# Moving every second one of the first twelve input loads from SyncE's queue to ScalarE's

## The chip, the core and the metric

The kernel runs on one core of a Trainium2 chip. The metric is the device time of one execution in microseconds; the time given for a version is the median of several runs. Beside the times there is one profiled execution, whose trace all durations here come from.

## The reference

Inputs are q, k, v, a_re and a_im, each of shape (4, 8, 768, 48) = (batch B, heads H, sequence S, head size D), and four weight matrices. The first half is a gated linear recurrence, the second half a gated feed-forward layer on its result:

```python
mag = sqrt(a_re**2 + a_im**2);  scale = minimum(mag, 0.999) / (mag + 1e-6)
for t in range(S):
    new_re = ar*S_re - ai*S_im          # ar, ai: a_re*scale, a_im*scale at time t
    new_im = ar*S_im + ai*S_re
    S_re, S_im = new_re + outer(k[t], v[t]), new_im
    y[t] = q[t] @ S_re
x = y, heads side by side: (3072, 384)
out = x + sigmoid(x @ w_res) * ((gelu(x @ w_gate) * (x @ w_val)) @ w_out)
```

w_gate and w_val are 384 x 1536, w_out is 1536 x 384, w_res is 384 x 384. All inputs and the output are float32.

## The kernel before

The sequence is cut into six chunks of 128 positions. A *unit* of work is one chunk of one batch, or the same chunk of two batches: unit 0 is batch 0, chunk 0; unit 1 is batch 1, chunk 0; unit 2 is batches 2 and 3, chunk 0; units 3 and 4 are chunk 1 of batches 0, 1 and of 2, 3; and so on, 14 units in all. For each unit three Python functions record steps:

- `prepare` loads `ar`, `ai`, `q`, `k`, `vf` (one load per batch and tensor, line 366), and takes the complex gates into logarithm and angle. On ScalarE it computes `la = Ln(ar)` (L387) and `t = Exp(-la)` (L388); then `t = t*ai` (L390) and `s = t*t` (L392 on ScalarE or L394 on VectorE), `s = Ln(s+1)` (L395), `la = 0.5*s + la` (L396, VectorE), then lh and ll (L399, L401). The angle is `t = Arctan(t)` (L426). The running sums over the chunk are matmuls with a triangular matrix (L352); an angle carry from the chunk before is added by a small DMA from GpSimd's queue (`t<-fr`, L432 and L438); the split parts are `th` (L327) and `tl` (L445). Sine, cosine and the exponentials follow on ScalarE (L416, L417, L470), then the features of q and k.
- `attend` does the attention-like products (L528, L540) and the state.
- `forward` does the feed-forward layer: the gate and value products on TensorE (L598), gelu on ScalarE (L603), the product on VectorE (L604), the output product (L624) and the store (L633).

A function `weights` records sixteen loads of the weight matrices, which GpSimd issues (L333), casting to bfloat16 on the way.

The steps are not run in the order of recording. `ORDER` is a list, written out by hand, of all step numbers; `Plan.run` walks it and lets each step emit its instruction. Each engine so gets its instructions in this order, and executes them in that order. `PLACE` maps some step numbers to an engine; the function `place(default)` looks up the number of the step that is about to be recorded. `Plan.run` also emits an activation table load for ScalarE (L640) whenever a step needs another table than the one in place. The first such load comes with the first step that computes on ScalarE, step 21, the logarithm of unit 0.

The order begins with loads only:

```python
    16, 97, 98, 17, 181, 178, 179, 294, 293, 410, 180, 411, 296, 295, 21, 22, 102, 103, 104, 105, ...
```

Steps 16 and 17 are `ar` and `ai` of unit 0; 97 and 98 those of unit 1; 178, 179 and 180, 181 those of unit 2 (two batches); 293, 294 are `ar` of unit 3 and 295, 296 its `ai`; 410, 411 are `ar` of unit 4. Steps 21 and 22 are unit 0's logarithm and exponential on ScalarE, 102 and 103 those of unit 1. The next loads after 295 in SyncE's order are 412 and 413 (`ai` of unit 4), 19, 100, 99, 643.

All wide work tiles, the loaded ones among them, share 25 buffers (`WD`). A load of a new tile takes the buffer whose last use lies furthest back in the order, and has to wait for that use. The first fourteen loads take fresh buffers. Load 412, the fifteenth, takes the one that held `s` of unit 0, whose last use is L396 of unit 0.

One load brings 128 positions x 8 heads x 48 floats, 192 KB, in pieces of 192 bytes (one position of one head).

Of the kernel before, what the change touches and what calls it, by code (L numbers as in the profile page):

```python
# [24 lines left out]


PLACE = {
    24: "DVE", 40: "DVE", 50: "DVE", 105: "DVE", 114: "DVE", 116: "POOL", 117: "POOL", 121: "DVE", 129: "ACT", 131: "DVE",
    145: "ACT", 190: "DVE", 213: "DVE", 223: "DVE", 225: "ACT", 230: "ACT", 236: "DVE", 305: "DVE", 306: "DVE", 322: "POOL",
    330: "DVE", 340: "DVE", 342: "ACT", 344: "DVE", 422: "DVE", 446: "DVE", 456: "DVE", 460: "DVE", 463: "ACT", 554: "POOL",  # L30
# [92 lines left out]
class Plan:  # L123
# [10 lines left out]
    def add(self, eng, kind, fn, reads=(), writes=(), size=1, act=None):  # L134
        deps = set()
        for v in reads:
            deps.update(v.writers)
        for v in writes:
            deps.update(v.writers)
            deps.update(v.readers)  # L140
        stores = [v.store for v in list(reads) + list(writes) if v.store is not None]
        stores = sorted(set(stores), key=stores.index)
        t = Step(eng, kind, fn, deps, stores, size, act)
        t.index = len(self.steps)
        for v in writes:
            v.writers, v.readers = [t], []
        for v in reads:
            if t not in v.writers:
                v.readers.append(t)
        for x in stores:  # L150
            x.users.append(t)
        self.steps.append(t)
        return t
# [25 lines left out]
def kernel(  # L179
# [13 lines left out]
    nc = tc.nc  # L193
# [123 lines left out]
    add = plan.add  # L317

    def place(default):

        return PLACE.get(len(plan.steps), default)

# [31 lines left out]
    def flat(t, n):  # L354
        return t[:, 0:n].rearrange("p c h d -> p (c h d)")

    def prepare(p):
        s, n = st[p], size[p]
        N = n * DM

        def load(name, src):
            s[name] = Wide(name, FP)
            parts = []
            for i, (b, c) in enumerate(units[p]):
                def fn(i=i, b=b, c=c):
                    nc.sync.dma_start(out=s[name].tile[:, i], in_=src[b, :, c * 128:(c + 1) * 128, :].rearrange("h t d -> t h d"))  # L366
                v_ = s[name].part()
                add("SP", "load", fn, (), [v_])
                parts.append(v_)
            s[name].writers = [x for v_ in parts for x in v_.writers]  # L370

# [3 lines left out]
        for name, src in (("ar", a_re), ("ai", a_im), ("q", q), ("k", k), ("vf", v)):  # L375
            load(name, src)
# [43 lines left out]
        if units[p][0][1] < NC - 1:  # L420
            add("POOL", "mrd", lambda: nc.gpsimd.dma_start(
                out=s["mr"].tile[0:n * H, 0, :], in_=P2("E")[127:128].rearrange("p c (h d) -> p (c h) d", d=D)), [s["E"]], [s["mr"]])
# [6 lines left out]
        if olds:  # L429
            src = sorted({where[(b, c - 1)] for b, c in units[p]})  # L430
            if len(src) == n == 2 and src[0][0] == src[1][0]:
                add("POOL", "carry", lambda u=src[0][0]: nc.gpsimd.dma_start(  # L432
                    out=F("t")[0:1], in_=st[u]["fr"].tile[127:128].rearrange("p c m -> p (c m)"), accum_op=OP.add), olds, [s["t"]])
            else:
                tp = [s["t"].part() for _ in range(n)]
                for i in range(n):
                    tp[i].writers, tp[i].readers = list(s["t"].writers), list(s["t"].readers)
                    add("POOL", "carry", lambda i=i, u=src[i]: nc.gpsimd.dma_start(  # L438
                        out=F("t")[0:1, i * DM:(i + 1) * DM], in_=st[u[0]]["fr"].tile[127:128, u[1]], accum_op=OP.add), [olds[i]], [tp[i]])
# [9 lines left out]
        for i, (b, c) in enumerate(units[p]):  # L449
            if ST:  # L450
                add("PE", "cumT", lambda i=i: sums(cth[i], i, F("th"), F("tl")), [s["th"], s["tl"]], [cth[i]])
            else:
# [5 lines left out]
                out=T("fr")[:, i], in0=T("fr")[:, i].bitcast(INT), scalar=-TWO_PI, in1=cth[i].tile,  # L458
# [10 lines left out]
        for m, (src, bi) in enumerate((("fr", zero), ("fw", half_pi))):  # L469
            act("sin", lambda m=m, src=src, bi=bi: nc.scalar.activation(  # L470
                out=T("CS")[:, 0:n * H, m, :], in_=P2(src).rearrange("p c (h d) -> p (c h) d", d=D),
                func=AF.Sin, bias=bi, scale=1.0 if m == 0 else -1.0), [s[src]], [cs[m]], "T")

        for g, src, mag in (("Q", "q", "E"), ("K", "k", "Ei")):
            add("DVE", "qe", lambda g=g, src=src, mag=mag: nc.vector.tensor_tensor(
                out=T(g + "e")[:, 0:n * H].rearrange("p x u d -> p (x u d)"), in0=flat(T(src), n),
                in1=P2(mag).rearrange("p c m -> p (c m)"), op=OP.mult), [s[src], s[mag]], [s[g + "e"]], n)
        for g in "QK":
            s[g] = Feat(g)
            add("DVE", "feat", lambda g=g: nc.vector.tensor_tensor(  # L480
                out=s[g].tile[:, 0:n * H, 0:DD].rearrange("p x (u d) -> p x u d", u=2),
                in0=T(g + "e")[:, 0:n * H].to_broadcast([128, n * H, 2, D]), in1=T("CS")[:, 0:n * H], op=OP.mult), [s[g + "e"]] + cs, [s[g]], n)
        s["QT"], s["KT"] = [], []
        for i in range(n):
            for g in "QK":
                s[g + "T"].append(Buf(g + "T"))
                gT = s[g + "T"][i]
                if p >= PE_T:
                    add("SP", "dT", lambda g=g, i=i, gT=gT: nc.sync.dma_start(
                        out=gT.tile, in_=s[g].tile[:, i * H:(i + 1) * H].rearrange("p x d -> p (x d)"), transpose=True), [s[g]], [gT])  # L490
# [180 lines left out]
```

## Time and profile before

| | |
|---|---|
| median of 3 runs | 268.33 us (265.72 to 268.8) |
| profiled execution: time / span on the core | 270.18 us / 268.4 us |
| mean granted TensorE clock | 0.973 |
| PE busy | 229.0 us (85%) |
| VectorE (DVE) busy | 231.7 us (86%) |
| ScalarE (ACT) busy | 218.8 us (82%) |
| GpSimd (POOL) busy | 103.8 us (39%) |
| DMA queue q1 (issued by SyncE) | 157,696 packets, 35.53 MB |
| DMA queue q0 (issued by GpSimd) | 4,448 packets, 3.90 MB |

The span is the time from the first to the last instruction on the core; the execution's own time is 1.8 us longer. "Busy" leaves out the instructions of an engine's sequencer: waiting, branching and issuing DMAs. An engine with a "q" behind its name (SPq, POOLq) is that sequencer. A releaser behind an arrow is what ended a wait.

### The profile page before, as it was taken

To read this page: it belongs to the slowest core of one execution; us is meant where nothing else is said; L and a number is where in the kernel's file an instruction comes from. 1 tells how busy PE (TensorE), PEld (TensorE's weight loads), DVE (VectorE), ACT (ScalarE), POOL (GpSimd) and SP (SyncE) were. 2 spreads that over 40 slices of the span, in tenths; PEclk is the share of its full clock that TensorE was granted. 3 is DMA by queue.
4 is the path that set the end of the run, shared out by engine and by line. 5 is a ranking of instruction groups with operands and counts; after the bars stand their busy time and mean duration, and the time that the engine had idled before them with its cause. 6 is when DMAs were issued, how large, how long until landed. Compare 5 with 4: busy or idle time off the path is not lost.

```text
span 268.4 us, 6355 instructions
## 1 busy us (share of the span) xinstructions
PE 229.0 (85%) x2426; PEld 183.2 (68%) x2426; DVE 231.7 (86%) x398; ACT 218.8 (82%) x356; POOL 103.8 (39%) x125
## 2 busy tenths in 40 slices
PE   0323857498996999999997999988999999999993
PEld 0112646397874988688876777777888868877782
DVE  3689899969996899999998999997999998829273
ACT  6999989778698999998999999998988868651240
POOL 1202247793131953768458855742110001201010
PEclk9999995989997999999999999999999999999999
DMA  8999999999819989977979999767896937420111
GB/s 141 188 185 187 188 179 190 208 180 201 143 26 176 156 140 178 180 159 146 192 178 168 192 186 174 165 106 173 175 186 142 153 72 176 91 56 29 46 62 59
DMA packets 162174, 39.83 MB, mean 148 GB/s; under 512 B 155616, under 2 KB 162144, under 8 KB 162144
## 3 DMA queue, kind: packets, MB, share of 16 engines
q1 hardware_dynamic: 157696, 35.53, 74.7%
q0 software_dynamic: 4448, 3.90, 9.1%
q8 instruction: 19, 0.31, 0.5%
q14 instruction: 11, 0.09, 0.1%
HBM read 31.26 MB, written 4.72 MB: 134 GB/s over the span
## 4 chain that ended last, share of the span: by engine, by line
PE 62%; DMA 15%; ACT 10%; POOL 5%; SPq 4%; issue 3%; DVE 1%; POOLq 0%; DVEq 0%; ACTq 0%
PE pb L598 29%; PE pb L624 14%; DMA ar<-in_a_re_dram 7%; PE pb L352 5%; PE pb L613 4%; SPq L366 4%; DMA t<-fr 3%; PE pb L528 3%; DMA wg<-in_moe_w_gate_dram 3%; PE pb L497 3%; ACT L640 2%; POOL th L327 1%; DMA KT<-fK 1%; ACT t L426 1%; ACT CS L470 1%
## 5 line engine op out<-in xcount | busy, mean ns | idle before, releaser
L598 PE MATMUL pb<-xT,wg 128*128 128x256 bf16 (+1 forms) x504 | 57.5, 264 | 5.8 <-ACT h L603 2.2
L604 DVE SCALAR_TENSOR_TENSOR h<-h,pb 128x512 bf16<-128x512 bf16 (+1 forms) x84 | 48.4, 602 | 16.1 <-ACT h L603 9.4
L603 ACT ACTIVATE h<-pb 128x512 bf16<-128x512 f32 (+1 forms) x84 | 41.0, 545 | 25.6 <-PE pb L598 25.4
L598 PE MATMUL pb<-xT,wv 128*128 128x256 bf16 (+1 forms) x504 | 57.1, 257 | 0.9 <-DMA wv<-in_moe_w_val_dram 0.9
L624 PE MATMUL pb<-wo,h 128*128 128x384 bf16 x288 | 56.2, 326 | 0.0
L640 ACT ACT_TABLE_LOAD x42 | 53.9, 1283 | 1.4 <-PEq L655 0.7
L598 PEld LDWEIGHTS <-wg 128*128 128x128 bf16 x504 | 44.9, 101 | 14.0 <-issue 3.9
L598 PEld LDWEIGHTS <-wv 128*128 128x128 bf16 x504 | 42.3, 98 | 8.2 <-DMA wv<-in_moe_w_val_dram 1.3
L631 POOL TENSOR_TENSOR ot<-ot,x 128x384 f32<-128x384 f32 x18 | 16.5, 921 | 53.6 <-DVE ot L628 41.3
L624 PEld LDWEIGHTS <-h 128*128 128x128 bf16 x288 | 26.5, 97 | 12.9 <-issue 0.5
L531 DVE TENSOR_TENSOR am<-pb,mask 128x512 bf16<-128x512 f32 x48 | 31.8, 681 | 2.3 <-PE pb L528 2.3
L390 POOL TENSOR_TENSOR t<-t,ai 128x768 f32<-128x768 f32 (+1 forms) x9 | 15.6, 1737 | 18.6 <-DMA ai<-in_a_im_dram 13.1
L528 PE MATMUL pb<-QT,KT 96*128 96x128 bf16 x192 | 17.4, 219 | 4.1 <-ACT QT L325 1.7
L352 PE MATMUL pb<-th,ut_one 128*128 128x384 f32 x24 | 11.7, 486 | 8.7 <-POOL th L327 8.7
L327 POOL CAST v<-vf 128x768 bf16<-128x768 f32 (+1 forms) x10 | 8.8, 878 | 23.7 <-DMA vf<-in_v_dram 14.7
L528 PEld LDWEIGHTS <-KT 96*128 96x128 bf16 x192 | 13.1, 97 | 7.1 <-issue 2.3
L445 POOL TENSOR_TENSOR tl<-t,th 128x768 fp32r<-128x768 f32 (+1 forms) x9 | 14.8, 1649 | 7.1 <-ACT th L325 6.8
L327 POOL CAST th<-t 128x768 fp32r<-128x768 f32 (+1 forms) x9 | 10.3, 1152 | 17.7 <-DMA t<-fr 6.2
L613 PE MATMUL pb<-wr,xT 128*128 128x384 bf16 x72 | 16.3, 343 | 0.0
L497 PE MATMUL pb<-ident,fK 128*128 128x128 bf16 x112 | 9.7, 242 | 6.9 <-DVE fK L480 6.9
L540 PE MATMUL pb<-v,am 128*128 128x48 bf16 x192 | 12.5, 186 | 2.8 <-DVE am L531 2.8
L387 ACT ACTIVATE la<-ar 128x768 f32<-128x768 f32 (+1 forms) x14 | 10.4, 759 | 5.5 <-DMA ar<-in_a_re_dram 4.6
(91 smaller groups left out, 484.9 us busy)
## 6 DMA issues: line engine op xcount, KB each, us to landing
ar<-in_a_re_dram SPq DMA_DIRECT2D x24, 192.0 KB, 4.6
ai<-in_a_im_dram SPq DMA_DIRECT2D x24, 192.0 KB, 4.5
k<-in_k_dram SPq DMA_DIRECT2D x24, 192.0 KB, 4.4
q<-in_q_dram SPq DMA_DIRECT2D x24, 192.0 KB, 4.3
vf<-in_v_dram SPq DMA_DIRECT2D x24, 192.0 KB, 4.3
out_dram<-ot SPq DMA_DIRECT2D x24, 192.0 KB, 2.3
wv<-in_moe_w_val_dram POOLq DMA_DIRECT2D x6, 192.0 KB, 6.0
wg<-in_moe_w_gate_dram POOLq DMA_DIRECT2D x6, 192.0 KB, 7.2
```

Of the source, the lines that this page charges most:

```text
L327: on[eng].tensor_copy(out=out, in_=in_)
L352: nc.tensor.matmul(out=bank.tile, lhsT=ut_one, rhs=x[:, i * DM:(i + 1) * DM], start=(j == 0), stop=(j == 1))
L497: nc.tensor.transpose(out=tp.tile[:, h, :], in_=s[g].tile[:, i * H + h], identity=ident)
L528: nc.tensor.matmul(out=ap.tile[:, h, :], lhsT=kT.tile[0:DD, u * H // 2 + h, :], rhs=qT.tile[0:DD, u * H // 2 + h, :], start=True, stop=True)
L531: add("DVE", "am", lambda u=u, am=am, ap=ap: nc.vector.tensor_tensor(out=am.tile[:, u * H // 2:(u + 1) * H // 2, :], in0=ap.tile, in1=mask ...
L598: nc.tensor.matmul(out=o_.tile[:, u, :], lhsT=w_[:, k_, (2 * m + u) * 128:(2 * m + u + 1) * 128], rhs=s["xT"].tile[:, k_, 0:n].rearrange(" ...
L603: add("ACT", "gelu", lambda gp=gp, hv=hv: nc.scalar.activation(out=hv(), in_=gp.tile, func=AF.Gelu), [gp], [hh], n, "G")
L604: add("DVE", "h", lambda vp=vp, hv=hv: nc.vector.scalar_tensor_tensor(out=hv(), in0=hv(), scalar=0.5, in1=vp.tile, op0=OP.mult, op1=OP.mul ...
L613: nc.tensor.matmul(out=rp.tile, lhsT=s["xT"].tile[:, k_, i, :], rhs=wr[:, k_, :], start=(k_ == 0), stop=(k_ == KF - 1))
L624: nc.tensor.matmul(out=op_.tile, lhsT=s["h2"].tile[:, k_, i * 128:(i + 1) * 128], rhs=wo[:, k_, :], start=(k_ == 0), stop=(k_ == NF - 1))
L631: add(e8, "otx", lambda i=i, ot=ot, e8=e8: on[e8].tensor_tensor(out=ot.tile, in0=ot.tile, in1=s["x"].tile[:, i].rearrange("p h d -> p (h d ...
L640: plan.run(ORDER, lambda table: nc.scalar.preload_act_table_set(ACT_SETS[table]))
```

## The change

Of the first twelve loads in the order, the 2nd, 4th, 6th, 8th, 10th and 12th (steps 97, 17, 178, 294, 410, 411) are issued with `nc.scalar.dma_start`, so from ScalarE's instruction stream and on ScalarE's DMA queue. The order list is the same; so are the transfers, the buffers and all other steps.

```diff
 PLACE = {
+    97: "ACT", 17: "ACT", 178: "ACT", 294: "ACT", 410: "ACT", 411: "ACT",
     24: "DVE", 40: "DVE", 50: "DVE", 105: "DVE", 114: "DVE", 116: "POOL", 117: "POOL", 121: "DVE", 129: "ACT", 131: "DVE",
...
             for i, (b, c) in enumerate(units[p]):
-                def fn(i=i, b=b, c=c):
-                    nc.sync.dma_start(out=s[name].tile[:, i], in_=src[b, :, c * 128:(c + 1) * 128, :].rearrange("h t d -> t h d"))
+                eq = place("SP")
+
+                def fn(i=i, b=b, c=c, eq=eq):
+                    (nc.scalar if eq == "ACT" else nc.sync).dma_start(out=s[name].tile[:, i], in_=src[b, :, c * 128:(c + 1) * 128, :].rearrange("h t d -> t h d"))
                 v_ = s[name].part()
-                add("SP", "load", fn, (), [v_])
+                add(eq, "load", fn, (), [v_])
                 parts.append(v_)
```

## The prediction

> **What bounds the kernel now.** I read the page first, its slices above all, then the chain that ended last, then the timeline of the first 16 us, then busy time by stage.
>
> The page, its rows for ACT, DMA and GB/s in 40 slices of 6.7 us:
>
> ```profile
> ACT  6999989778698999998999999998988868651240
> DMA  8999999999819989977979999767896937420111
> GB/s 141 188 185 187 188 179 190 208 180 201 143 26 176 156 140 178 180 159 146 192 178 168 192 186 174 165 106 173 175 186 142 153 72 176 91 56 29 46 62 59
> ```
>
> Up to about 70 us the DMA engines are at nine tenths with 180 to 208 GB/s: the stage is bound by transfers, and ScalarE is at nine tenths beside it. The chain that ended last, in order of time (start, duration, what), shows how the two are linked:
>
> ```profile
> 1.87 0.84 SPq L366
> ...
> 10.89 4.58 DMA ar<-in_a_re_dram
> 15.55 0.84 ACT la L387
> ...
> 38.36 1.81 POOL t L390
> ...
> 44.45 7.86 DMA wg<-in_moe_w_gate_dram
> ...
> 53.44 1.32 PE pb L598 x12
> 55.62 14.28 DMA ar<-in_a_re_dram
> 69.98 0.85 ACT la L387
> ```
>
> The chain runs through SyncE's issues to the twelfth load (10.89), through ScalarE (15.55), GpSimd and the weights that it issues, TensorE's first gate products (53.44) and a load that took 14.28 us. After that it is mostly TensorE.
>
> The timeline from 0 to 16 us (start, duration, engine, line; in brackets the idle time before):
>
> ```profile
> 0.74 1.28 ACT L640 ACT_TABLE_LOAD   x1 [0.74 <-PEq L655]
> 0.74 1.07 SPq L366 DMA_DIRECT2D ar<-in_a_re_dram  x2
> 3.87 0.52 ACT L387 ACTIVATE la<-ar 128x384 f32<-128x384 f32 x1 [1.84 <-DMA ar<-in_a_re_dram]
> 10.89 1.00 SPq L366 DMA_DIRECT2D ar<-in_a_re_dram  x1
> 11.93 4.11 SPq L366 DMA_DIRECT2D ai<-in_a_im_dram  x4
> 15.55 0.84 ACT L387 ACTIVATE la<-ar 128x768 f32<-128x768 f32 x1 [0.54 <-DMA ar<-in_a_re_dram]
> ```
>
> Here the reader sees the main thing: an issue isn't free. SyncE's first two take 0.53 us each, the later ones about 1.03 (4.11 / 4). That is the time in which 192 KB move at 190 GB/s, so the issuing sequencer is held until the engines have taken earlier loads. Busy time by stage (PE, PEld, DVE, ACT, POOL, each with its count, clock, DMA share, GB/s):
>
> ```profile
> 4.00:16.00 12.00, 2.90 (x6) 1.39 (x6) 7.80 (x15) 10.80 (x17) 1.79 (x2) 1.00 1.31 189
> 16.00:28.00 12.00, 4.38 (x16) 2.96 (x17) 11.02 (x19) 11.95 (x18) 1.93 (x2) 1.00 1.37 186
> 54.00:70.00 16.00, 15.14 (x225) 13.69 (x224) 13.03 (x23) 11.28 (x28) 8.85 (x12) 0.93 1.19 192
> 83.00:268.00 185.00, 178.20 (x1901) 142.50 (x1900) 161.31 (x270) 147.34 (x245) 69.82 (x72) 0.99 0.74 140
> ```
>
> ScalarE works 22.75 of the 24 us from 4 to 28: it has next to no room there. After 83 us TensorE has 6.8 us of idle time in 185.
>
> **What the change removes.** Six issues leave SyncE. The transfers stay, and they are what paces SyncE, so I take nothing for this. What SyncE could gain is bounded by ScalarE's waits on `ar` loads, 0.54 us at 15.55 and 2.2 us at 69.98, so 2.8 us in all; at the other end it is nothing.
>
> The Trainium skill, "DMA: Bandwidth & Descriptors", section "Issuing engines are not separate DMA queues", says that DMAs from ScalarE and SyncE run on the same 16 engines and interleave, and that a second issuer only saves issue time, usually small beside the transfer. The first half agrees with the nine tenths above. The second doesn't agree with the 1.03 us of an issue: with issues as small as the rule has them the sum would be that of the second rival, 269.2, in place of 275.3.
>
> **What it adds.** Six issues on ScalarE, all ahead of its first table load and logarithm, since ScalarE works in the order of the list. The trace has no DMA issue on ScalarE, so I bound it by SyncE's rows.
> - Low: all six at the 0.53 us of the first two: 0.74 + 6 x 0.535 = 3.95 us.
> - High: the two sequencers share one line, and ScalarE's sixth issue ends where the twelfth ends now: 10.89 + 1.00 = 11.89 us.
> - Value: two quick issues, then four held back. With two queues sharing the engines each gets a load per 2 x 1.03 us: 0.74 + 1.07 + 4 x 2.06 = 10.05 us. That two queues share is seen where GpSimd's weights run: SyncE's row of two issues there takes 7.25 us in place of 2.1, in the answer for SyncE's timeline:
>
> ```profile
> 41.58 7.25 SPq L366 DMA_DIRECT2D q<-in_q_dram  x2
> ```
>
> The table load (1.28 us, now hidden ahead of the first load's landing) loses its cover and follows: 10.05 + 1.28 + 0.03 = 11.36 us for the logarithm that now starts at 3.87. ScalarE begins 7.5 us late. All inputs of the first units have landed by then, so the wait of 0.54 us at 15.55 goes: ScalarE is 7.0 us late from there on.
>
> **Where the stall goes.** Next late are the loads. The fifteenth (step 412) takes the buffer of `s` of unit 0, which L396 frees; VectorE's timeline around 12 us, and SyncE's around 14:
>
> ```profile
> 12.05 0.56 DVE L396 SCALAR_TENSOR_TENSOR la<-s,la 128x384 f32<-128x384 f32 x1 [1.51 <-ACT s L395]
> 14.07 0.93 SPq L366 DMA_DIRECT2D ai<-in_a_im_dram  x1
> ```
>
> The buffer is free at 12.61, 1.46 us before the issue at 14.07. L396 waits for ScalarE's L395, so it moves with ScalarE: 412 goes out 7.5 - 1.46 = 6.0 us late, with all loads behind it in SyncE's queue, and the transfers that were the bound stand still for about that time. So the transfers don't absorb the delay. The weights don't either: GpSimd issues them behind L390 at 38.36, which waits for ScalarE's exponential (L388), so TensorE's first products at 53.44 are late by the 7.0 us too. At 69.98 ScalarE now waits 2.2 us for a load; if transfers are late by 6.0 only, 1.0 us of the 7.0 comes back there, at the most 2.2. I take nothing back, because later loads wait for buffers with less room than 1.46 (L401 frees one at 29.33, and the load goes out at 29.36). After 83 us the 6.8 us of TensorE's idle time belong to the same chain of engines, all late alike.
>
> **Sum:** +7.5 - 0.54 = +7.0 us. The profiled execution's own 270.18 us (span 268.4) becomes 277.2; it was 1.85 us above the median of the runs, and from that median, 268.33, I get 275.3 us. About 2% is what a measurement of this kernel can tell from no change: 5.4 us, so the line is at 273.7.
>
> **Rivals.**
> 1. One line for both sequencers. ScalarE is held to 11.89 us: logarithm at 13.20, 9.3 us late, less 0.54: +8.8, 277.1 us. For it: the depth of what a sequencer may have outstanding is seen for one issuer only. Against it: GpSimd's queue went on while SyncE's was held.
> 2. Light issue. ScalarE's queue takes six loads without holding it: 3.95 + 1.31 = 5.26, 1.4 us late, less 0.54: +0.85, 269.2 us; the 1.46 us of room at step 412 then hides it from the loads. For it: the 0.53 us of the first two. Against it: SyncE is held from its third issue on.
> 3. The delay is made up before 70 us. ScalarE is idle 4.7 us between 54 and 70 and 1.7 us between 40 and 54; if half of these 6.4 us can be closed, +3.8, 272.1 us. It needs TensorE's first products no later than some 56 to 57 us. Against it: the weights hang on ScalarE by way of L390.
> 4. Not slower: two queues move more. In the transfers' own view of the first 20 us (slices of 0.5 us) the rate is 249 GB/s for one slice, then about 190:
>
> ```profile
> GB/s 0 0 0 23 146 249 220 203 196 189 186 200 204 166 158 201 223 194 171 199 183 194 178 196 183 200 178 188 191 189 183 190 176 178 193 192 187 189 188 169
> ```
>
> If two queues hold 249, twelve loads need 0.79 in place of 1.03 us each, 2.9 us less. With light issue, 1.4 us late, and ScalarE's 2.8 us of waits on loads gone: -1.4, 266.9 us. It decides if both hold: over 220 GB/s in the first 12 us, and ScalarE's logarithm before about 6 us. Against it: 190 GB/s with one queue while the engines' share is already above 1. By the rule of the skill cited above this is excluded.
>
> That the change doesn't do what it says I leave out: none of the 114 other loads' step numbers stands in `PLACE`, so just these six move.
>
> **How the numbers follow.** Forecast 0.52, rival 1 0.18, rival 2 0.13, rival 3 0.11, rival 4 0.06. The likeliest is 275.3; its own range, from a sixth issue ending between 8.5 and 11.5 us and up to 1 us given back, is 273 to 277. The range for 8 in 10 takes in rival 1 above and most of rival 2 below: 268.6 to 278.3. Slower by over 2%: 0.46 of the forecast, 0.18 of rival 1, 0.02 of rival 3, so 0.66. Faster by over 2% would need 5.4 us, twice what all waits on loads are worth: 0.02. Within 2%: 0.32.
>
> **What would show it.** Right: six issues on ScalarE, the first two about 0.5 us, the others about 2 us, ending near 10 us; its table load behind them, the logarithm near 11.4; a hole of about 6 us in the transfers between 15 and 22 us; the first L598 near 60 in place of 53.4. Wrong: issues on ScalarE of 0.5 us throughout; no hole; step 412 still out by 15 us; more than 220 GB/s in the first 12 us; or the first L598 before 57.

## The result: slower, by twice the forecast

| | median | runs | profiled execution: time / span |
|---|---|---|---|
| before | 268.56 us | 4, 265.72 to 279.29 | 270.18 / 268.4 us |
| after | 282.35 us | 4, 281.61 to 283.98 | 281.92 / 280.1 us |

The ratio is 1.0559, 95% interval 1.0458 to 1.066. The forecast was 275.3 us, the range 268.6 to 278.3: the sign was right, the loss is 13.8 us by the medians in place of 7.0. The ratios, here and below, leave out executions more than 1.5% above the fastest of their kernel, as the 279.29 us here. Lines of `kernel.py` are 3 higher after the change (L366 is L369, L598 is L601); in each experiment they are that kernel's own.

**The first 60 us went as forecast.** ScalarE's timeline of the kernel after (start, duration, engine and line):

```profile
0.73 0.49 ACTq L369 DMA_DIRECT2D ar<-in_a_re_dram  x1
1.26 0.72 ACTq L369 DMA_DIRECT2D ai<-in_a_im_dram  x1
2.01 7.83 ACTq L369 DMA_DIRECT2D ar<-in_a_re_dram  x4
9.87 1.28 ACT L643 ACT_TABLE_LOAD   x1 [9.87 <-issue]
11.17 0.52 ACT L390 ACTIVATE la<-ar 128x384 f32<-128x384 f32 x1
```

Two issues of 0.49 and 0.72 us, then four that take 7.83 us together. The sixth ends at 9.84, the table load stands bare behind it, and the logarithm starts at 11.17: 7.30 us later than before. Further on, the timelines of SyncE and of TensorE:

```profile
19.79 0.99 SPq L369 DMA_DIRECT2D ai<-in_a_im_dram  x2
```

```profile
59.43 2.52 PE L601 MATMUL pb<-xT,wg 128*128 128x128 bf16 x42
```

Step 412 goes out at 19.79 in place of 14.07, 5.7 us late, and TensorE's first long group of L601 starts at 59.43; the timeline of before has that group, of L598 there, at 53.24 (the chain's row of 53.44 lies in it), so it is 6.2 late. The page's slices show the hole between: 66 GB/s in the third, where there were 185, and more such gaps later (14 in the fifteenth).

```profile
ACT  0599999978999729987999996999998968851240
DMA  9959999999919909976996999867799945330111
GB/s 143 187 66 197 186 153 188 206 206 205 170 32 176 135 14 200 173 156 118 141 216 132 195 169 176 167 145 159 144 190 203 155 87 142 86 82 27 46 59 57
```

**Most of the second half of the loss arises near 92 us.** VectorE's timeline there, of the kernel before and of the kernel after:

```profile
86.86 0.95 DVE L475 TENSOR_TENSOR Qe<-q,E 128x768 bf16<-128x768 f32 x1
87.72 1.18 DVE L560 TENSOR_TENSOR Gb<-U,M 96x384 bf16<-96x384 f32 x1
88.82 0.94 DVE L480 TENSOR_TENSOR fQ<-Qe,CS 128x1536 bf16<-128x1536 bf16 x1
```

```profile
90.30 1.57 DVE L478 TENSOR_TENSOR Qe<-q,E 128x768 bf16<-128x768 f32 x1
91.80 5.55 DVE L563 TENSOR_TENSOR Gb<-U,M 96x384 bf16<-96x384 f32 x1
97.28 0.94 DVE L483 TENSOR_TENSOR fQ<-Qe,CS 128x1536 bf16<-128x1536 bf16 x1
```

The same small product `Gb`, 0.54 us when nothing is beside it, took 5.55 us. GpSimd's timelines, again before and after, tell what ran meanwhile:

```profile
87.09 1.40 POOL L327 CAST v<-vf 128x768 bf16<-128x768 f32 x1 [5.98 <-DMA vf<-in_v_dram]
88.44 1.41 POOL L327 COPY mr<-mr 16x48 f32<-16x48 f32 x1
89.82 0.90 POOL L631 TENSOR_TENSOR ot<-ot,x 128x384 f32<-128x384 f32 x1
```

```profile
89.95 1.12 POOL L328 CAST v<-vf 128x768 bf16<-128x768 f32 x1 [5.51 <-DMA vf<-in_v_dram]
91.01 0.94 POOL L328 COPY mr<-mr 16x48 f32<-16x48 f32 x1
91.93 0.90 POOL L634 TENSOR_TENSOR ot<-ot,x 128x384 f32<-128x384 f32 x1
...
96.12 0.82 POOL L568 TENSOR_TENSOR Gf<-U,M 96x384 f32<-96x384 f32 x1
```

Seven GpSimd instructions run without a gap from 89.95 to 96.94. Behind the cast VectorE comes through once, with `Qe`: it takes 1.57 us where others of its form take 0.95, and the copy beside it 0.94 where others take 0.21. `Gb` then stands through the other five, from 91.93 to 96.94, and comes through 0.4 us after the last. Before, `Qe` (86.86) had started 0.23 us ahead of the cast (87.09); `Gb` and `fQ` both came through while the copy stood, and GpSimd's next five began only at 89.82. After, the cast (89.95) is 0.35 us ahead of `Qe` (90.30). TensorE's matmuls stand behind `fQ`:

```profile
98.28 1.89 PE L500 MATMUL pb<-ident,fQ 128*128 128x128 bf16 x16 [5.27 <-DVE fQ L483]
```

By stages (stretch, its length, then busy time of PE, PEld, DVE, ACT, POOL), 85 to 125 us, before and after:

```profile
85.00:125.00 40.00, 40.00 (x449) 32.74 (x448) 38.51 (x62) 37.63 (x60) 26.03 (x24) 0.98 0.97 166
```

```profile
85.00:125.00 40.00, 32.72 (x329) 26.42 (x328) 38.98 (x48) 32.93 (x52) 18.81 (x17) 0.96 0.90 149
```

TensorE was busy all 40 us before and 32.72 after, while VectorE was counted busy for 38.98 us with 48 instructions done in place of 62: some 9 us of its time went into waiting inside instructions (`Qe` and `Gb` above, `lh` and `Ke` below), which the profile counts as work.

The Trainium skill, "SBUF — State Buffer", section "Who interferes with whom", has a mechanism for such rows: a VectorE instruction with two SBUF inputs and a GpSimd instruction that reads SBUF want the same ports, which one of them locks for the whole instruction, and the order of issue decides who stands. The trace agrees that one of the two stands, and, where `Qe` meets the cast, that it is the later one (by 0.35 us). It doesn't agree throughout, as far as starts in the profile tell: `Gb` started at 91.80, 0.13 us ahead of GpSimd's next instruction (91.93), and stood all the same, through five instructions and not one. That it is these ports was not isolated by a run here.

### The profile page after: what moved, and what is told of

Same layout as the page of the kernel before. It is cut to its first block, busy times and chain, and to the rows that moved or that the text cites. A ratio compares the mean times of both kernels' runs of the same rounds, so it can differ in the third digit from the quotient of the medians.

```text
span 280.1 us, 6353 instructions
## 1 busy us (share of the span) xinstructions
PE 227.6 (81%) x2426; PEld 181.9 (65%) x2426; DVE 243.0 (87%) x398; ACT 218.0 (78%) x356; POOL 112.9 (40%) x125
## 3 DMA queue, kind: packets, MB, share of 16 engines
q10 hardware_dynamic: 6240, 1.18, 3.1%
## 4 chain that ended last, share of the span: by engine, by line
PE 43%; DVE 16%; issue 5%; ACT 3%; DMA 3%; DVEq 0%; SPq 0%
PE pb L601 22%; PE pb L627 11%; PE pb L616 2%; PE pb L353 2%; PE pb L531 2%; DVE h L607 2%; DVE Ke L478 2%; DMA xT<-x 2%; DVE lh L402 1%; DMA k<-in_k_dram 1%; ACT CS L473 1%; DVE fQ L483 1%; DVE ll L404 1%; PE pb L500 1%; DVE am L534 1%
## 5 line engine op out<-in xcount | busy, mean ns | idle before, releaser
L601 PE MATMUL pb<-xT,wg 128*128 128x256 bf16 (+1 forms) x504 | 55.6, 257 | 3.6 <-DVE h L607 1.4
L601 PE MATMUL pb<-xT,wv 128*128 128x256 bf16 (+1 forms) x504 | 57.4, 259 | 0.3 <-ACT E L419 0.2
L601 PEld LDWEIGHTS <-wg 128*128 128x128 bf16 x504 | 43.1, 98 | 11.4 <-issue 2.2
L601 PEld LDWEIGHTS <-wv 128*128 128x128 bf16 x504 | 42.6, 98 | 7.9 <-issue 2.1
L328 POOL CAST th<-t 128x768 fp32r<-128x768 f32 (+1 forms) x9 | 11.4, 1276 | 24.3 <-ACT t L429 13.2
L531 PE MATMUL pb<-QT,KT 96*128 96x128 bf16 x192 | 18.0, 225 | 3.4 <-ACT Ei L420 1.7
L393 POOL TENSOR_TENSOR t<-t,ai 128x768 f32<-128x768 f32 (+1 forms) x9 | 16.3, 1812 | 10.3 <-ACT t L391 5.3
L531 PEld LDWEIGHTS <-KT 96*128 96x128 bf16 x192 | 13.7, 101 | 6.2 <-issue 2.1
L328 POOL CAST v<-vf 128x768 bf16<-128x768 f32 (+1 forms) x10 | 9.5, 948 | 18.9 <-DMA vf<-in_v_dram 9.9
L353 PEld LDWEIGHTS pb<-th,ut_one 128*128 128x128 f32 x24 | 5.1, 214 | 17.3 <-POOL th L328 16.3
L419 ACT ACTIVATE E<-pb 128x384 f32<-128x384 f32 x24 | 11.8, 494 | 5.6 <-PE pb L353 5.6
L478 DVE TENSOR_TENSOR Qe<-q,E 128x768 bf16<-128x768 f32 (+1 forms) x14 | 15.8, 1130 | 0.0
L616 PE MATMUL pb<-wr,xT 128*128 128x384 bf16 x72 | 15.3, 326 | 0.6 <-DMA wr<-in_moe_w_res_dram 0.6
```

What stands on the lines that cost most here:

```text
L328: on[eng].tensor_copy(out=out, in_=in_)
L353: nc.tensor.matmul(out=bank.tile, lhsT=ut_one, rhs=x[:, i * DM:(i + 1) * DM], start=(j == 0), stop=(j == 1))
L531: nc.tensor.matmul(out=ap.tile[:, h, :], lhsT=kT.tile[0:DD, u * H // 2 + h, :], rhs=qT.tile[0:DD, u * H // 2 + h, :], start=True, stop=True)
L601: nc.tensor.matmul(out=o_.tile[:, u, :], lhsT=w_[:, k_, (2 * m + u) * 128:(2 * m + u + 1) * 128], rhs=s["xT"].tile[:, k_, 0:n].rearrange(" ...
L616: nc.tensor.matmul(out=rp.tile, lhsT=s["xT"].tile[:, k_, i, :], rhs=wr[:, k_, :], start=(k_ == 0), stop=(k_ == KF - 1))
```

## The experiments

The theory (A in the expectations, with changing figures): the six issues make ScalarE start 7.3 us late, and this is carried; on top of it the moved instants decide collisions between VectorE and GpSimd, each worth up to 5 us. The rivals: the second queue, or issuing from ScalarE as such, has a price of its own (B, later D); or the late start explains the whole (C). A collision is called lost where a VectorE instruction stands for microseconds. Times that lie far apart are given singly. The four groups e1 to e4, e6 to e9, e10 to e13 and e14 to e16 ran on a chip each, on which the kernel before had 265.81, 267.36, 270.11 and 271.02 us.

**e1_tables7: the late start without a moved load.** The kernel before, with seven table loads more on ScalarE ahead of its first logarithm:

```diff
+    for i in range(7):
+        nc.scalar.preload_act_table_set(ACT_SETS["TG"[i % 2]])
     plan.run(ORDER, lambda table: nc.scalar.preload_act_table_set(ACT_SETS[table]))
```

> The kernel before, all loads on SyncE, with seven more table loads on ScalarE ahead of its first logarithm (7 x 1.29 us), so that this starts near 11.1 us as in the changed kernel (11.17). Theory A (the late start of ScalarE is the only cause; where the time goes is decided later): 279 to 285 us, with VectorE held for some 5 us behind GpSimd near 92 us. Theory B (two DMA queues side by side change which loads land when): 268 to 272. Theory C (a late start is carried to the end as it is): 275 to 276.

273.36 us (271.57, 280.46, 273.1, 273.62) against 265.81, ratio 1.0256 (1.0166 to 1.0346). The logarithm started at 11.05, and step 412 went out at 19.67, as late as in the changed kernel, with all loads on one queue: the hole in the transfers follows from ScalarE's late start, not from the queues. The profiled execution (271.57) has no VectorE instruction held for 5 us at 92 us: `Qe` came at 91.17, the cast at 91.27. So a late start of 7.2 us cost 5.8 there, and 7.3 and 7.8 in the two executions near it; what the one of 280.46 lost no trace shows. None of the three expected ranges holds the median.

**e2_gpsimd6: the six loads on GpSimd's queue.** ScalarE issues nothing.

```diff
-    97: "ACT", 17: "ACT", 178: "ACT", 294: "ACT", 410: "ACT", 411: "ACT",
+    97: "POOL", 17: "POOL", 178: "POOL", 294: "POOL", 410: "POOL", 411: "POOL",
```

> The six loads go to GpSimd's queue in place of ScalarE's; GpSimd has nothing else to do until 7.9 us, and ScalarE issues nothing. Theory A: ScalarE starts within 2 us of the kernel before, so 266 to 272 us. Theory B: a second queue beside SyncE's is enough for the loss, 278 to 285.

278.34, 277.45, 277.07 and 267.08 us, against 265.81. The logarithm started at 3.95. In the profiled execution (278.34) `Gb` took 5.56 us at 87.01, the cast at 85.42 having come 0.09 us ahead of `Qe`. So the collision can be lost without any delay of ScalarE. The execution of 267.08, of which there is no trace, shows that two queues can cost next to nothing; the other three lie 5 us above theory A's range and near B's.

**e3_after_noburst and e4_before_noburst: fewer GpSimd instructions in a row.** The five steps behind the copy of `mr` go to other engines, in the kernel after (e3) and before (e4):

```diff
-    ... 671: "POOL", ... 786: "POOL", ...
+    176: "DVE", 357: "DVE", 367: "DVE",
+    ... 671: "DVE", ... 786: "ACT", ...
```

> The changed kernel, with the GpSimd steps of the burst near 92 us on other engines (L634 once, L568 twice and L448 once on VectorE, L328 of th on ScalarE). Theory A: VectorE's 5.55 us instruction becomes 0.6, and the time falls to 272 to 277 us although VectorE has 2.6 us more to do. Theory C (the delay is plain and has no place): 281 to 285.

> The kernel before with the same five steps moved off GpSimd: what that edit does by itself. Theory A: no burst held VectorE there, so 267 to 271 us, and the distance to the changed kernel with the same edit shrinks from 14 us to 3 to 7. Theory C: the distance stays 12 to 14.

e3: 281.32 us, ratio 1.0574 (1.0489 to 1.0658), which misses theory A's 272 to 277; e4: 275.79, ratio 1.0405 (1.0305 to 1.0505). `Gb` took 0.57 us in e3, so the run of GpSimd instructions was what had held it. But the edit costs 10 us by itself, and a kernel that is 10 us slower can't show where 14 went. Their distance, 5.5 us, is less than the change's 13.8, and in A's range of 3 to 7; no more is read from the pair.

**e6_after_vlate and e8_before_vlate: the cast comes later.** Load 530 (`q`) ahead of 419 and 418 (`vf`) in `ORDER`, so that the `vf` that releases the cast lands about 1 us later; in the kernel after (e6) and before (e8):

```diff
-    ... 544, 254, 419, 418, 530, 533, ...
+    ... 544, 254, 530, 419, 418, 533, ...
```

> The changed kernel with one load of q (step 530) ahead of the two loads of v of unit 4 (419, 418) in SyncE's order, so that 418 lands 1 us later, GpSimd's cast of v (L328) starts behind VectorE's Qe (L478) and no longer 0.35 us ahead of it. Theory A (some 5 us are the late start of ScalarE, the rest is VectorE held for 5 us because GpSimd's cast came first): 271 to 276 us, and no instruction of VectorE over 3 us near 92 us. Theory C (the late start explains all, the held instruction is a symptom): 281 to 284.

> The kernel before with the same order of loads as in e6_after_vlate: what that edit does by itself. Theory A: the cast came second anyway, so 264 to 268 us in every execution, and the changed kernel with the same edit is 5 to 8 us slower than this.

e8: 266.39 us over ten runs (264.16 to 267.96), ratio 0.9983 (0.9934 to 1.0031); the kernel before had one execution of 278.55 among 13 on that chip, e8 none. e6: 276.74, 272.45, 278.56, 277.55, one of four in A's range. Its `Gb` took 0.55 us; the hold at 92 us is gone. But GpSimd was held by VectorE elsewhere, in GpSimd's timeline of e6:

```profile
155.15 5.33 POOL L324 CAST v<-vf 128x768 bf16<-128x768 f32 x1
```

Eight VectorE instructions start one behind the other from 155.24 to 159.72, and this cast stood until 160.48, though it had started 0.09 us ahead of the first of them. The angle carry that GpSimd issues next went out at 160.43. Against e8, VectorE in e6 is 5 to 8 us late up to 168 us, which is the late start, 9 to 11 from 174 on and 10.0 at the end.

**e7_before_held: the collision without the change.** The kernel before, with four small memsets of an unused tile ahead of `Qe` (step 449). Planned were 0.6 us of VectorE; in the trace `Qe` starts 0.86 us behind the first of them:

```diff
+                if held:                     # step 449 only
+                    for _ in range(4):
+                        nc.vector.memset(ut_f, 0.0)
                 nc.vector.tensor_tensor(... in0=flat(T(src), n), in1=P2(mag)..., op=OP.mult)
```

> The kernel before, with four small memsets of an unused tile on VectorE (0.6 us together) ahead of the same Qe (L475 there), so that it starts after GpSimd's cast of v and not 0.23 us before it. ScalarE and all loads start as before. Theory A: VectorE's next instruction is held for some 5 us, and 0.6 us of work cost 8 to 11 us: 274 to 278 us. Theory C: 266 to 268.

276.36 us (272.06, 279.1, 275.45, 277.27) against 267.36, ratio 1.0272 (1.0124 to 1.0421). In the profiled execution (272.06) the loss is 4.7 us. Timelines of VectorE and of GpSimd in e7:

```profile
83.46 0.94 DVE L478 MEMSET ut_f<- 128x128 f32 x4
84.32 5.82 DVE L479 TENSOR_TENSOR Qe<-q,E 128x768 bf16<-128x768 f32 x1
```

```profile
83.28 0.89 POOL L327 CAST v<-vf 128x768 bf16<-128x768 f32 x1 [5.73 <-PE pb L603]
84.12 0.21 POOL L327 COPY mr<-mr 16x48 f32<-16x48 f32 x1
84.31 0.90 POOL L636 TENSOR_TENSOR ot<-ot,x 128x384 f32<-128x384 f32 x1
...
88.50 0.82 POOL L570 TENSOR_TENSOR Gf<-U,M 96x384 f32<-96x384 f32 x1
```

The cast and the copy were through when `Qe` came, and `Qe` took 5.82 us, through the five GpSimd instructions from 84.31 to 89.32. ScalarE's logarithm was at 4.01 and the loads are the same. 0.9 us of work, placed here, costs 9 us by the medians and 7.3 by the ratio: the collision is shown by itself.

**e9_tables4: half the late start.** Four table loads in e1's edit; the logarithm at 7.18, 3.3 us late.

> The kernel before with four more table loads on ScalarE ahead of its first logarithm, which so starts near 7.2 us, 3.3 us late. Theory A: the late start alone costs 1 to 4 us, 267 to 270 us, unless GpSimd's cast comes first, then 275 to 279. Theory C: 14 us for 7.3 us late would be 6 us here, 272.

280.24, 270.71, 277.88, 270.78 us, against 267.36. The profiled execution (280.24) has `Gb` at 88.64 with 5.55 us and a cast at 160.81 with 5.34. The two of 270.7 and 270.8 are 3.4 us above the kernel before, about as much as the late start; that the collisions were won there is argued, not traced.

**e10_after_both and e11_before_both: the cast at 155 us moved as well.** e6 and e8, with step 921 (that cast) put behind the carry 1231, just ahead of 1232:

```diff
-    ... 806, 715, 921, 621, ... 814, 812, 1232, 811, ...
+    ... 806, 715, 621, ... 814, 812, 921, 1232, 811, ...
```

> e6_after_vlate with one more edit: GpSimd's cast of v (step 921), which in that run stood 4.5 us behind VectorE at 155 us and made the angle carry behind it late, comes after that carry in the order (before step 1232). Theory A (a late start of 7.3 us costs 5 to 7 us; each place where VectorE and GpSimd stand behind each other costs more): 270 to 274 us in every execution, none at 276 or above. Theory C (no such places; the time is the late start's own): 276 to 283.

> The kernel before with both order edits (two loads of v one place later, the cast of step 921 behind the carry): what they do by themselves. Theory A: 263 to 268 us in every execution, 5 to 8 us below e10_after_both.

e11: 266.29 us (263.91 to 266.94), ratio 0.9884 (0.9781 to 0.9987) against the 270.11 that the kernel before had on this chip (264.5 to 274.3, by how its collisions went). e10: 277.37 (275.41 to 278.99), ratio 1.0309 (1.02 to 1.0418); the 270 to 274 us that the theory gave were missed, and the time lies in theory C's range. No hold above 3 us was left, and e10 still stood 11 us behind e11, where 5 to 8 were expected.

**e12_two_on_act: two of the six.** e10 with steps 97 and 17 alone on ScalarE.

> As e10_after_both, but only the first two of the six loads (steps 97 and 17) on ScalarE. It is through with them near 2 us and with its table load near 3.3, before the first load lands at 3.8. Theory A: no late start, 263 to 268 us, the same as e11_before_both within 2 us. Theory B (a second queue beside SyncE's does the harm): 1 to 4 us above e11_before_both.

266.38 us (265.39 to 267.34), as e11's 266.29 on the same chip. The logarithm started at 4.34, 0.45 us late. For two loads, issuing from ScalarE on a second queue has no price that could be seen; a price comes with issues that are held.

**e13_gpsimd_both: e10 with the six on GpSimd.** The line of e2, in e10.

> As e10_after_both, but the six loads on GpSimd's queue in place of ScalarE's. Theory A: ScalarE starts near 4 us, 263 to 269 us, and the second value of e2_gpsimd6 (277 to 278 us) is gone. Theory B: 270 to 278.

265.74, 273.75, 274.52, 273.57 us. The first, which is the profiled one, is e11's time: a second queue for these loads needn't cost anything. Where the other three, which lie in theory B's range, lost theirs no trace shows.

**e14 to e16: does e10's rest belong to the late start?** e11 with seven (e14) or four (e15) table loads ahead of the first logarithm, and e10 with four loads on ScalarE (e16):

```diff
-    97: "ACT", 17: "ACT", 178: "ACT", 294: "ACT", 410: "ACT", 411: "ACT",
+    97: "ACT", 17: "ACT", 178: "ACT", 294: "ACT",
```

> The kernel before with both edits of the order, and seven table loads more on ScalarE ahead of its first logarithm, which then starts at about 11.05 us, some 7.2 late, with all loads on SyncE's queue. Theory A (the change costs its late start, and what VectorE and GpSimd then lose to each other at their new instants, nothing else): the same order and the same late start as the kernel with six loads on ScalarE and both edits (277.4 us), so 266.3 + 7.2 = 273.5 us and up to 5 more for collisions, 273 to 279 us; the part above 273.5 is to be found as VectorE instructions stretched by GpSimd between 95 and 170 us. Theory D (issuing six loads from ScalarE costs about 4 us of its own beside the late start): 272.5 to 274.5 us, and step by step earlier than the kernel with six loads on ScalarE from the first 60 us on.

> The same with four table loads more: logarithm at about 7.2 us, 3.3 late. Theory A: 266.3 + 3.3 = 269.6 us, with collisions up to 275, not below 268.5. A second form of it, that collisions only come with more than some 5 us of delay, would give 269.6 +- 1. Theory D: 268.6 to 270.6 us.

> Both edits of the order, the 2nd, 4th, 6th and 8th load on ScalarE (steps 97, 17, 178, 294), the 10th and 12th on SyncE: by the issues of the kernel with six, 0.48 + 0.74 + about 1.4 + 1.9, ScalarE is free near 5.2 us and the logarithm starts near 6.6, 2.7 late. Theory A: 266.3 + 2.7 = 269.0 us and up to 5 for collisions, near the kernel with four table loads. Theory D: 4 of 6 of the extra 4 us, 269.0 + 2.7 = 271.7 us, about 2 above the kernel with four table loads.

e14: 272.58 us (270.23 to 274.07), 6.3 above the 266.29 of e11, which ran earlier and on another chip. Step by step it stands where e10 stands, within 0.1 us at the logarithm and at the first running sums (15.75 and 15.65), within 0.7 us from there, and with `Qe` at 99.63 and 99.64. The hole is there too, with nothing issued by ScalarE, in the third slice of e14's page:

```profile
GB/s 147 187 70 188 187 156 189 200 205 215 202 35 113 189 159 173 183 142 169 151 215 149 193 153 199 164 92 184 141 188 161 174 69 166 85 68 29 46 61 58
```

The time is the one that theory D gave (272.5 to 274.5), but D's other half, that e10 would be behind from the first 60 us on, is refuted. Then VectorE of e14 and of e10:

```profile
99.63 0.95 DVE L471 TENSOR_TENSOR Qe<-q,E 128x768 bf16<-128x768 f32 x1
```

```profile
99.64 2.93 DVE L474 TENSOR_TENSOR Qe<-q,E 128x768 bf16<-128x768 f32 x1
...
107.56 2.11 DVE L479 TENSOR_TENSOR fK<-Ke,CS 128x1536 bf16<-128x1536 bf16 x1
109.59 1.17 DVE L559 TENSOR_TENSOR Gb<-U,M 96x384 bf16<-96x384 f32 x1
110.69 1.68 DVE L398 TENSOR_SCALAR lh<-la 128x768 fp32r<-128x768 f32 x1
```

GpSimd's `tl` came at 99.91 in e10 and at 100.10 in e14, in both after `Qe`; in e10 `Qe` stood until `tl` was through, in e14 it did not. Against their usual 0.94, 0.94, 0.54 and 0.54 us, e10's four instructions lost 1.99 + 1.17 + 0.63 + 1.14 = 4.9 us, and VectorE works back to back here: the next step (`fr`) stands 4.93 us behind e14's. That is e10's distance to e14, 4.8 us. In e14 none of them was stretched, and the median lies 0.4 us below the 273 to 279 of theory A.

e15: 267.35 us (265.45 to 268.48), below the 268.5 that I had as the floor. It starts 3.2 us late, and its VectorE is still 2.3 late at 92 us; but e11's own trace has `lh` at 100.04 with 2.17 us and `Ke` at 108.17 with 2.68, and e15's has neither, so it is 0.6 late after the first and 1.2 us early after the second. e16: 266.34, 275.88, 273.62, 271.18 us, its logarithm at 6.49, 2.6 us late; the profiled execution (266.34) has no VectorE instruction stretched by more than 1.5 us. Its median, 272.4, lies near theory D's 271.7, but the spread of 9.5 us in one kernel doesn't let it decide.

Two things stand beside the theory. GpSimd stood in single instructions for 4.38 us in e11's trace, 4.37 in e8's and 4.40 and 4.32 in e16's, all of executions of 266 us; so a hold of GpSimd by itself need not cost anything. In e6 the carry waited behind it. And with both edits in the order, the kernels with four or six loads on a second queue (e10, e13, e16) had ten of twelve executions at 271 us or above, and those with all loads on SyncE (e11, e14, e15) three of twelve, all in e14. That a second queue makes lost collisions more frequent is thus not excluded.

## Why the prediction was right in part and wrong in size

- **Six issues on ScalarE: right.** End at 10.05 forecast, 9.84 measured (0.49, 0.72, then 7.83 for four); logarithm at 11.36 forecast, 11.17 measured. The rule of the Trainium skill weighed there ("DMA: Bandwidth & Descriptors", section "Issuing engines are not separate DMA queues"), that issue time is usually small, did not hold for the third to the sixth load, 1.96 us each beside a median of 7.8 us to landing; its other half, that a second issuer brings no bandwidth, agrees with the traces: 161 GB/s over the first 12 us after the change, 162 before.
- **Step 412 and the hole: right.** 6.0 us forecast, 5.7 measured. e1 and e14, with all loads on SyncE, show that it hangs on ScalarE alone.
- **First L598 near 60: right for the long group**, 59.43. The 53.44 us that the prediction took for TensorE's first products is the chain's row; single L598 products start at 49.72 before and at 56.92 after. Taken by these, the sign "before 57" would have counted against the forecast, although they are late by 7.2 us.
- **"After 83 us ... all late alike": this step failed.** The sum carried +7.0 us to the end as one shift. The late start by itself does cost about that: 6.3 us (e14 against e11), 5.8 to 7.8 (three of e1's four executions). What is missing is a term for VectorE and GpSimd holding each other, which changes when all instants shift. Against e8's trace, where `Gb` isn't held, TensorE after the change is 6.1 us late where e8 stands at 53.6 and 6.7 where it stands at 62.8, then 12.1 at the transposes of `fQ` (98.28 against 86.17), 13.7 at e8's 88.6, 16.6 at its 109.3 and 15.4 at the end of the span (280.1 against 264.7). So some 7 us of the loss are the forecast and 5.4 are `Qe` and `Gb`. The next 1.6 are TensorE's own: after 5.27 us of idle time the granted clock was 0.54 from 98 to 101 us, and the sixteen transposes of `fQ` took 1.89 us in place of e8's 1.06. The rest is two more VectorE instructions beside GpSimd, 0.55 and 0.95 us in e8; 1.2 us come back by the end:

```profile
113.33 2.18 DVE L402 TENSOR_SCALAR lh<-la 128x768 fp32r<-128x768 f32 x1
...
121.47 2.68 DVE L478 TENSOR_TENSOR Ke<-k,Ei 128x768 bf16<-128x768 f32 x1
```

- The signs of this were in the profile of before and I read past them: `Gb` at 87.72 with 1.18 us where others of its form take 0.54, and GpSimd's copy of a 16 x 48 tile taking 1.41 us at 88.44.
- **The rivals.** The high bound for the issues (rival 1), light issue (rival 2) and more bandwidth from two queues (rival 4) are refuted by the first 12 us; the delay was not made up before 70 us (rival 3). None had the collisions, and my upper end, 278.3, was set to take in rival 1, so the range ended below the result.
- **What stays open.** Which collisions are lost is known after the fact, from each trace; no run shows a rule by which it could have been told beforehand. A shift of 0.2 to 0.9 us went with it in e7, e10 and e14. Whether loads on a second queue make lost collisions more frequent is open too.

The two edits of the order don't make the change worthwhile, but e8 and e11 take the kernel before's worst executions away: 266.4 and 266.3 us, none above 268, against up to 278.55 and 274.3 on the same chips.

## What to carry to other kernels

Here a DMA issue held the engine that issued it, 0.5 us at first and 1.96 us once transfers were queued; ahead of an engine's first computation, move only as many as start at once (two here, free; six, 7.3 us). When all instants of a tight schedule shift, the shift is not a bound of the estimate: 7.3 us late cost 6 to 15 here, and 3.3 us late 1 to 13. Look for instructions that take longer than others of their form, count what such collisions cost where they are lost, and put that into the range. Before explaining a remainder, impose the delay without the change (here by idle table loads), and see whether the remainder comes with it.

## What the runs showed of the hardware

- VectorE stood for 5.55 us in an instruction of 0.54 while five GpSimd instructions ran back to back, and GpSimd 5.33 us in a cast that takes 0.82 while eight VectorE instructions did: one engine was kept out through a whole run of the other's instructions, not only through one. Which one stood didn't follow from the starts alone: in e6 the cast (155.15) stood behind `Gb` (155.24), in e10 `Qe` (99.64) behind `tl` (99.91).
- This time is counted as busy: VectorE's 243.0 us after the change and 231.7 before are the same 398 instructions.
- Four held issues of 192 KB on ScalarE took 1.96 us each with SyncE issuing beside it, against 1.03 on SyncE alone; all loads together moved no faster than from one queue (161 and 162 GB/s over the first 12 us).
- After 5.27 us without a matmul, TensorE's granted clock was 0.54 for the next 3 us.
